# Signs of the weight words on VectorE, a folded factor for w_out, and layer 2's magnitude on ScalarE

## The chip, the cores and the metric

One core of one Trainium2 chip runs the whole program. The metric is device time in microseconds, the median of several runs. A profiled execution of the kernel before gives the trace that is read below. TensorE multiplies matrices, VectorE (DVE in the trace) and ScalarE (ACT) work on elements from PSUM and SBUF, GpSimd (POOL) on elements in SBUF, SyncE (SP) issues the DMAs.

## The reference

Attention over 4 batches, 8 heads, 576 positions and head size 64 (four heads see a local window of 32, four see every 32nd position), then two feed-forward layers over 2304 tokens of 512 values with 2048 hidden values each:

```python
attn = softmax(where(mask, q @ k.T / sqrt(64), -1e9)) ; x = attn @ v      # (2304, 512)
h = x @ moe_w_in  ; g = maximum(0.01 * h, h)                     ; x = g @ moe_w_out
h = x @ moe2_w_in ; g = maximum(h, 0) + log1p(exp(-abs(h)))      ; out = g @ moe2_w_out
```

q, k and v are float32. The four weights come as float64 and are read as pairs of 32-bit words.

## The kernel before

**Products.** Each operand of the feed-forward products is cut into a float16 high part and a float16 remainder, and a product is three matmuls (`mm3`, L462 to L464: high by high, high by remainder, remainder by high). Layer 1 runs over 8 units of 288 tokens: a first product (`plan_first`, pairs of 128 hidden rows) whose result ScalarE bends (L483) and casts (L486) and whose remainder GpSimd makes (L489), and a second product (`plan_second`, or for unit 0 `plan_second_by_f`, which goes along the hidden rows as the quarters of w_out come). Layer 2 runs over 9 units of 256 tokens, each in 8 steps k: first product, `size`, `relu`, `soft`, `add`, `sums`, `cut_high`, `cut_rest`, second product. Its second product uses seven products in place of eight, from sums of blocks.

**Weights.** A weight comes in four quarters of 2 MB, q = 0 to 3. `largest` (L156, VectorE) takes a quarter's largest magnitude, which goes over TensorE to all partitions and gives a scale. `low` (L162, VectorE) shifts the low words down by 29 bits, `shift` (L209, ScalarE) scales the high words, `merge` (L214, VectorE) joins both to a float32, `high` (L221, ScalarE) casts it to float16 and the remainder is the difference: `rest` (L226, on GpSimd for W1, on VectorE for W2) or `rest_of` (L230, VectorE). A sign bit has to be put into each low word before the merge: for W1 and O1 by ScalarE after the shift (`sign_of_scaled`, L205, float16 written with a stride of four), for W2 and O2 by VectorE before the shift (`sign`, L198). W1's and W2's quarters have a scale each (`plan_quarter`); O1's and O2's have one scale for all four quarters, so O1's conversion starts after its last quarter has come (`plan_together`). The loads of O1's quarters go into the areas that W1's quarters leave, one by one. The hidden values of layer 1 keep W1's four scales, and O1's quarters are multiplied with factors that even them out: `high` takes the factor as the scale of its cast, `rest_of` as the scalar of its difference.

**Layer 2's gate.** `size` (L1136, VectorE) clears the sign bit of h in PSUM, so SBUF holds the unscaled magnitude; `relu` (L1143, ScalarE) reads the same PSUM tile, after `size`, and frees it; `soft` (L1150, L1151, ScalarE) takes the exponent with the negative scales `nsc`, and then the logarithm.

**Order.** Every instruction is emitted by a planner (`Plan.run`): it keeps a clock for each engine, with a cost written beside each step, and one more clock, "port", for GpSimd's steps and the VectorE steps marked `port=True`. Among the steps that could start within 0.5 us of the earliest it takes the one of lowest rank. `RANKS` has an offset and a slope for each kind of step: A0 to A3 and B0 to B3 attention, L and LW and LO loads, W1r, W1m, O1r and O1m conversion, G0 to G2 first products of units 0 to 2, S0 to S2 their second products, M the later units, F, Fa, Fd, S, X and E layer 2. The order on each engine is fixed by this; at run time each engine goes through its queue in order. Where the plan sees TensorE free before 130 us it puts in filler matmuls (L92).

Of the kernel before, what the change touches and what calls it, by code (L numbers as in the profile page):

```python
# [10 lines left out]
F16 = mybir.dt.float16  # L11
F32 = mybir.dt.float32
I32 = mybir.dt.int32
U32 = mybir.dt.uint32
U16 = mybir.dt.uint16
AF = mybir.ActivationFunctionType
ALU = mybir.AluOpType
# [4 lines left out]
B, H, S, D = 4, 8, 576, 64  # L22
# [33 lines left out]
def build(tc, qt, kl, ks, v, wi1, wo1, wi2, wo2, mloc, mstr, out):  # L56
    nc = tc.nc
    with ExitStack() as ctx:
# [79 lines left out]
        flat = lambda y: y.rearrange("p a b -> p (a b)")  # L138


        class Weight:
# [60 lines left out]
            def sign_of_scaled(self, q):  # L202

                w = self.t[q].bitcast(F16).rearrange("p s (n t) -> p s n t", t=4)
                nc.scalar.activation(w[:, :, :, 1], self.words(q)[1].bitcast(F32), AF.Copy)  # L205

# [13 lines left out]
            def high(self, q, hl, by=1.0):  # L220
                nc.scalar.activation(flat(hl[0]), self.f[q], AF.Copy, scale=by)  # L221
                self.hl[q] = hl
# [4 lines left out]

            def rest_of(self, q, by):
                hi, lo = self.hl[q]
                nc.vector.scalar_tensor_tensor(  # L230
                    out=flat(lo), in0=self.f[q], scalar=by, in1=flat(hi), op0=ALU.mult, op1=ALU.subtract
                )
# [354 lines left out]
        W1, O1, W2, O2 = Weight("i1", wi1), Weight("o1", wo1), Weight("i2", wi2), Weight("o2", wo2)  # L587
# [26 lines left out]
        plan = Plan({"mm": 2, "sc": 1, "pt": 1, "po": 1, "s": 4, "a": 3, "t": 3, "qk": 5, "rs": 2, "x2": 2, "gr": RING, "ob": 2}, idle, 130.0)  # L614
# [85 lines left out]
        def plan_together(W, name, after, parts, then, w1):  # L700
# [6 lines left out]
            for q in range(4):  # L707
                ld = plan.add("SP", 5.9, lambda q=q: W.load(q, area(q)), after[q], ("L" + name, q))
                big = step("DVE", 2.2, lambda q=q: W.largest(q, m()[:, q : q + 1]), [ld], q)
                low = step("DVE", 1.14, lambda q=q: W.low(q), [ld], q + 0.1, port=True)  # L710
                loads.append(big)
                read.append([big, low])
# [15 lines left out]
            for q in range(4):  # L728
                y = step("ACT", 2.07, lambda q=q: W.shift(q, st["s"]), [t] + read[q], 4 + q)
                y = step("ACT", 1.9, lambda q=q: W.sign_of_scaled(q), [y], 4 + q)  # L730
                y = step("DVE", 2.2, lambda q=q: W.merge(q), [y], 4 + q, port=True)
                y = step("ACT", 1.85, lambda q=q: W.high(q, parts(q), O1.by[:, q : q + 1]), [y] + made[-1:] * (q % 2), 4 + q)
                made.append(
                    step("DVE", 2.3, lambda q=q: W.rest_of(q, O1.by[:, q : q + 1]), [y], 4 + q, port=True)
                )
            return made, scaled

        def plan_quarter(W, name, q, place, after, parts, after_read, then=None, eng="DVE"):
# [22 lines left out]
            if not then:  # L761
                y = step("DVE", 2.35, lambda: W.sign(q), [y], 0.2, port=True)
            y = step("ACT", 2.07, lambda: W.shift(q, st["s"]), [sc, x, y], 0.3)
            if then:
                y = step("ACT", 1.9, lambda: W.sign_of_scaled(q), [y], 0.3)
# [307 lines left out]
        class Unit:  # L1073
# [34 lines left out]
            def scales(self):  # L1108
                new = lambda n, t: sml.tile([P, n], F32, name=t, tag=t)
                self.sc, self.nsc = new(4, "x2s"), new(4, "x2n")  # L1110
# [3 lines left out]
                nc.vector.tensor_scalar(out=self.nsc, in0=self.sc, scalar1=-1.0, scalar2=None, op0=ALU.mult)  # L1114
# [19 lines left out]
            def size(self, k):  # L1134
                t = self.a[k] = tmp.tile([P, 2, U1], F32, name="t", tag="t")[:, :, :U2]
                nc.vector.tensor_scalar(  # L1136
                    out=t.bitcast(I32), in0=self.ps[k].bitcast(I32), scalar1=0x7FFFFFFF, scalar2=None, op0=ALU.bitwise_and
                )
# [9 lines left out]
            def soft(self, k):  # L1148
                a = self.a[k]
                nc.scalar.activation(a, a, AF.Exp, scale=self.nsc[:, k // 2 : k // 2 + 1])  # L1150
                nc.scalar.activation(a, a, AF.Ln, bias=1.0)  # L1151
# [75 lines left out]
        for u in range(NU2):  # L1227
# [9 lines left out]
            for k in range(NK):  # L1237
# [5 lines left out]
                size = plan.add("DVE", 0.6, bind(U.size), [g1], rank("Fd", k), take=["t"])  # L1243
# [96 lines left out]
```

## Time and profile before

| | us |
|---|---|
| median of 3 runs | 870.89 |
| runs | 870.03 to 873.74 |
| profiled execution | 871.47 |
| its span, first to last instruction | 869.5 |
| TensorE busy | 831.9 (96%) |
| VectorE busy | 533.7 (61%) |
| ScalarE busy | 528.3 (61%) |
| GpSimd busy | 265.0 (30%) |

The mean granted clock of TensorE is 0.995 of full speed. Busy time holds an instruction from its start to its end; where VectorE and GpSimd exclude each other, the time that one is held up lies in its duration. "L205" is line 205 of the kernel before.

### The profile page before, as it was taken

To read this page: it belongs to the slowest core of one execution; us is meant where nothing else is said; L and a number is where in the kernel's file an instruction comes from. 1 tells how busy PE (TensorE), PEld (TensorE's weight loads), DVE (VectorE), ACT (ScalarE), POOL (GpSimd) and SP (SyncE) were. 2 spreads that over 40 slices of the span, in tenths; PEclk is the share of its full clock that TensorE was granted. 3 is DMA by queue.
4 is the path that set the end of the run, shared out by engine and by line. 5 is a ranking of instruction groups with operands and counts; after the bars stand their busy time and mean duration, and the time that the engine had idled before them with its cause. 6 is when DMAs were issued, how large, how long until landed. Compare 5 with 4: busy or idle time off the path is not lost.

```text
span 869.5 us, 17639 instructions
## 1 busy us (share of the span) xinstructions
PE 831.9 (96%) x7330; PEld 684.6 (79%) x7330; DVE 533.7 (61%) x1232; ACT 528.3 (61%) x938; POOL 265.0 (30%) x194
## 2 busy tenths in 40 slices
PE   9888798799999999999999999999999999999997
PEld 5556576578777777787777777888888888888886
DVE  4895652542033535049647859977787778677684
ACT  5899979933456542263726457757575666657572
POOL 2365753120332124140504124323222322223131
PEclk9999999999999999999999999999999999999999
DMA  8932320121013470013221120000000000000000
GB/s 329 390 126 112 140 98 1 67 81 56 1 58 138 158 304 25 2 41 154 98 97 29 71 98 1 26 2 25 2 25 2 25 2 26 1 26 1 26 25 25
DMA packets 10991, 63.27 MB, mean 73 GB/s; under 512 B 1344, under 2 KB 1440, under 8 KB 7840
## 3 DMA queue, kind: packets, MB, share of 16 engines
q1 hardware_dynamic: 10656, 62.00, 19.0%
q8 instruction: 57, 0.93, 0.4%
q10 hardware_dynamic: 256, 0.16, 0.1%
q14 instruction: 22, 0.18, 0.1%
HBM read 57.44 MB, written 4.72 MB: 71 GB/s over the span
## 4 chain that ended last, share of the span: by engine, by line
PE 69%; ACT 12%; DVE 11%; DMA 3%; issue 3%; POOL 1%; SPq 0%; DVEq 0%; ACTq 0%; POOLq 0%
PE h L462 11%; PE h L464 11%; PE h L463 11%; PE o L462 10%; PE o L464 10%; PE o L463 10%; ACT pair L205 3%; ACT pair L209 2%; DMA pair<-wo_dram 2%; ACT s L368 2%; PE ps L322 2%; DVE pair L1005 2%; PE po L419 2%; PE pt L399 1%; ACT t L483 1%
## 5 line engine op out<-in xcount | busy, mean ns | idle before, releaser
L462 PE MATMUL h<-x,w 128*128 128x256 f16 (+1 forms) x1088 | 303.5, 279 | 7.2 <-ACT t L483 5.0
L464 PE MATMUL h<-x,w 128*128 128x256 f16 (+1 forms) x1088 | 303.4, 279 | 4.3 <-POOL w L226 4.3
L463 PE MATMUL h<-x,w 128*128 128x256 f16 (+1 forms) x1088 | 303.4, 279 | 0.0
L1155 POOL TENSOR_TENSOR pair<-pair,t 128x512 f32<-128x512 f32 x72 | 100.4, 1394 | 268.6 <-ACT t L1151 171.1
L489 POOL TENSOR_TENSOR g<-t,g 128x576 f16<-128x576 f32 x64 | 104.3, 1633 | 183.7 <-ACT g L486 181.7
L462 PE MATMUL o<-g,pair 128*128 128x288 f16 x512 | 147.7, 288 | 2.8 <-ACT pair L221 1.8
L464 PE MATMUL o<-g,pair 128*128 128x288 f16 x512 | 147.6, 288 | 2.5 <-DVE pair L230 2.5
L463 PE MATMUL o<-g,pair 128*128 128x288 f16 x512 | 147.5, 288 | 0.0
L463 PEld LDWEIGHTS <-w 128*128 128x128 f16 x1088 | 106.5, 98 | 27.3 <-issue 8.7
L464 PEld LDWEIGHTS <-w 128*128 128x128 f16 x1088 | 106.4, 98 | 24.3 <-POOL w L226 5.2
L462 PEld LDWEIGHTS <-w 128*128 128x128 f16 x1088 | 106.4, 98 | 19.4 <-issue 0.2
L1167 ACT ACTIVATE gr<-pair,x2b 128x896 f16<-128x896 f32 x72 | 74.0, 1038 | 57.2 <-DVE pair L1163 57.2
L1171 DVE SCALAR_TENSOR_TENSOR gr<-pair,x2b,gr 128x896 f16<-128x896 f32 x72 | 86.4, 1209 | 24.8 <-ACT gr L1167 24.7
L1163 DVE TENSOR_TENSOR pair<-pair 128x128 f32<-128x128 f32 x288 | 80.2, 324 | 16.8 <-POOL pair L1155 14.3
L1143 ACT ACTIVATE pair<-h,x2s 128x512 f32<-128x512 f32 x72 | 49.0, 680 | 60.0 <-DVE t L1136 54.4
L464 PE MATMUL o<-w,gr 128*128 128x256 f16 x306 | 83.4, 273 | 0.9 <-DVE gr L1171 0.7
L462 PE MATMUL o<-w,gr 128*128 128x256 f16 x306 | 83.4, 273 | 0.0
L463 PE MATMUL o<-w,gr 128*128 128x256 f16 x306 | 83.4, 273 | 0.0
L390 POOL TENSOR_TENSOR s<-s,sm 96x512 f32<-96x512 f32 (+3 forms) x48 | 43.7, 931 | 121.4 <-DVE sm L385 64.1
L483 ACT ACTIVATE t<-h,gs 128x576 f32<-128x576 f32 x64 | 47.0, 735 | 49.0 <-PE h L464 48.8
L1136 DVE TENSOR_SCALAR t<-h 128x512 int32<-128x512 int32 x72 | 48.7, 685 | 29.0 <-PE h L464 28.4
L214 DVE SCALAR_TENSOR_TENSOR pair<-pair 128x2048 int32<-128x2048 int32 x16 | 37.4, 2338 | 45.9 <-ACT pair L205 35.3
(123 smaller groups left out, 1391.1 us busy)
## 6 DMA issues: line engine op xcount, KB each, us to landing
pair<-wo_dram SPq DMA_DIRECT2D x12, 2048.0 KB, 7.8
pair<-wi_dram SPq DMA_DIRECT2D x8, 2048.0 KB, 10.1
out_dram<-pair SPq DMA_DIRECT2D x18, 256.0 KB, 2.2
q<-qt_dram SPq DMA_DIRECT2D x12, 288.0 KB, 5.9
v<-v_dram SPq DMA_DIRECT2D x2, 1408.0 KB, 7.7
pair<-v_dram SPq DMA_DIRECT2D x2, 1408.0 KB, 6.0
k<-ks_dram SPq DMA_DIRECT2D x7, 288.0 KB, 3.3
k<-kl_dram SPq DMA_DIRECT2D x5, 304.0 KB, 3.8
```

The lines of the kernel that those rows point to most:

```text
L390: nc.gpsimd.tensor_tensor(out=sv, in0=sv, in1=rs, op=ALU.mult)
L462: nc.tensor.matmul(ps, ah, bh, start=first, stop=False)
L463: nc.tensor.matmul(ps, ah, bl, start=False, stop=False)
L464: nc.tensor.matmul(ps, al, bh, start=False, stop=last)
L483: nc.scalar.activation(t, ps, AF.Prelu, scale=gates[f // 4], alpha=0.01)
L489: nc.gpsimd.tensor_tensor(out=g[:, 1, f : f + 2, :], in0=t, in1=g[:, 0, f : f + 2, :], op=ALU.subtract)
L1136: nc.vector.tensor_scalar(out=t.bitcast(I32), in0=self.ps[k].bitcast(I32), scalar1=0x7FFFFFFF, scalar2=None, op0=ALU.bitwise_and)
L1143: nc.scalar.activation(r[:, :4].rearrange("p (j h) n -> p j (h n)", j=2), self.ps[k], AF.Relu, scale=self.sc[:, k // 2 : k // 2 + 1],)
L1155: nc.gpsimd.tensor_tensor(out=r, in0=r, in1=self.a[k], op=ALU.add)
L1163: nc.vector.tensor_tensor(out=r[:, o], in0=r[:, x], in1=r[:, y], op=op)
L1167: nc.scalar.activation(self.a[k][:, 0], self.r[k][:, 1:], AF.Copy, scale=self.ag)
L1171: nc.vector.scalar_tensor_tensor(out=a[:, 1], in0=self.r[k][:, 1:], scalar=self.ag, in1=a[:, 0], op0=ALU.mult, op1=ALU.subtract)
```

## The change

Five things change. `sign_of_scaled` goes, and W1 and O1 get `sign` on VectorE between `low` and `shift` (for O1's last quarter with a rank behind the scale). For O1 `high` no longer takes the factor: a new ScalarE step `fold` multiplies the merged float32 in place, `high` casts the product, and `rest` on GpSimd takes the place of `rest_of` on VectorE. In layer 2 `size` becomes a Prelu with slope -1 on ScalarE that reads PSUM and applies the unit's scale, so that `soft` needs the scale -1.0 only and the vector `nsc` goes; its step now also waits for the unit's scales. All 36 entries of `RANKS` have new numbers.

```diff
-    "Fa": (61.151, 23.937), "Fd": (809.007, 5.868), "G1": (1158.664, 0.271), "O1m": (1374.727, 1.358),
-    "S0": (1133.607, 120.000), "W1m": (975.007, 5.818), "W1r": (1347.663, 2.158), ...
+    "Fa": (411.724, 0.050), "Fd": (63.172, 34.443), "G1": (1489.548, 0.577), "O1m": (1411.571, 1.167),
+    "S0": (376.286, 13.166), "W1m": (932.785, 55.840), "W1r": (1390.426, 33.062), ...
...
+            def fold(self, q, by):
+                nc.scalar.activation(self.f[q], self.f[q], AF.Copy, scale=by)
...
-                read.append([big, low])
+                sign = step("DVE", 2.35, lambda q=q: W.sign(q), [low], q + 0.2 + 0.86 * (q == 3), port=True)
+                read.append([big, sign])
...
                 y = step("ACT", 2.07, lambda q=q: W.shift(q, st["s"]), [t] + read[q], 4 + q)
-                y = step("ACT", 1.9, lambda q=q: W.sign_of_scaled(q), [y], 4 + q)
                 y = step("DVE", 2.2, lambda q=q: W.merge(q), [y], 4 + q, port=True)
-                y = step("ACT", 1.85, lambda q=q: W.high(q, parts(q), O1.by[:, q : q + 1]), [y] + made[-1:] * (q % 2), 4 + q)
-                made.append(step("DVE", 2.3, lambda q=q: W.rest_of(q, O1.by[:, q : q + 1]), [y], 4 + q, port=True))
+                y = step("ACT", 1.8, lambda q=q: W.fold(q, O1.by[:, q : q + 1]), [y], 4 + q)
+                y = step("ACT", 1.85, lambda q=q: W.high(q, parts(q)), [y] + made[-1:] * (q % 2), 4 + q)
+                made.append(step("Pool", 4.1, lambda q=q: W.rest(q, nc.gpsimd), [y], 4 + q))
...
-            if not then:
-                y = step("DVE", 2.35, lambda: W.sign(q), [y], 0.2, port=True)
+            y = step("DVE", 2.35, lambda: W.sign(q), [y], 0.2, port=True)
             y = step("ACT", 2.07, lambda: W.shift(q, st["s"]), [sc, x, y], 0.3)
-            if then:
-                y = step("ACT", 1.9, lambda: W.sign_of_scaled(q), [y], 0.3)
...
             def size(self, k):
-                nc.vector.tensor_scalar(out=t.bitcast(I32), in0=self.ps[k].bitcast(I32), scalar1=0x7FFFFFFF, ...
+                nc.scalar.activation(t, self.ps[k], AF.Prelu, scale=self.sc[:, k // 2 : k // 2 + 1], alpha=-1.0)
...
-                nc.scalar.activation(a, a, AF.Exp, scale=self.nsc[:, k // 2 : k // 2 + 1])
+                nc.scalar.activation(a, a, AF.Exp, scale=-1.0)
...
-                size = plan.add("DVE", 0.6, bind(U.size), [g1], rank("Fd", k), take=["t"])
+                size = plan.add("ACT", 0.6, bind(U.size), [g1, scaled], rank("Fa", k), take=["t"])
```

## Rows read from the trace of the kernel before

**Rows 1.** stretches, us: PE, PEld, DVE, ACT, POOL busy, clock, DMA, GB/s
```profile
53.20:154.60 101.40, 87.38 (x776) 67.72 (x777) 58.35 (x176) 91.51 (x143) 60.86 (x37) 1.00 0.26 96
...
154.60:177.80 23.20, 18.98 (x132) 13.87 (x132) 14.50 (x8) 23.17 (x40) 0.24 (x1) 0.85 0.18 63
...
177.80:500.00 322.20, 320.74 (x2780) 255.72 (x2778) 147.42 (x343) 149.19 (x309) 87.88 (x66) 1.00 0.24 88
...
500.00:550.00 50.00, 46.05 (x410) 39.57 (x409) 40.52 (x60) 31.59 (x41) 17.00 (x9) 1.00 0.12 43
...
550.00:862.50 312.50, 312.50 (x2865) 280.15 (x2863) 232.51 (x547) 194.07 (x269) 83.38 (x64) 1.00 0.04 15
```

**Rows 2.** what TensorE waited for: total us, times, longest
```profile
PE po L419 <- ACT a L407: 5.3, 5, 2.2
...
PE h L462 <- ACT t L483: 5.0, 5, 1.9
...
PE h L464 <- POOL w L226: 4.3, 3, 2.2
...
PE o L464 <- DVE pair L230: 2.5, 1, 2.5
```

**Rows 3.** groups by shape, ScalarE: busy us, mean ns | idle before
```profile
L205 ACT ACTIVATE pair<-pair 128x2048 f16<-128x2048 f32 x8 | 38.3, 4784 | 0.1
...
L209 ACT ACTIVATE pair<-pair,s 128x2048 f32<-128x2048 f32 x12 | 26.4, 2200 | 8.6 <-DVE s L188 8.5
...
L221 ACT ACTIVATE w<-pair 128x2048 f16<-128x2048 f32 x8 | 15.2, 1902 | 5.9 <-DVE pair L214 5.9
```

**Rows 4.** timeline, start and duration in us, stages A and B
```profile
49.09 4.08 POOL L226 TENSOR_TENSOR w<-pair,w 128x2048 f16<-128x2048 f32 x1 [10.13 <-ACT w L221]
...
105.65 4.09 POOL L226 TENSOR_TENSOR w<-pair,w 128x2048 f16<-128x2048 f32 x1 [0.18 <-ACT w L221]
...
127.11 2.18 ACT L209 ACTIVATE pair<-pair,s 128x2048 f32<-128x2048 f32 x1
...
175.48 2.34 DVE L230 SCALAR_TENSOR_TENSOR pair<-pair,by_o 128x2048 f16<-128x2048 f32 x1
```

**Rows 5.** single lines: count, ns min/median/max, first and last start
```profile
L162 DVE TENSOR_SCALAR pair<-pair x16: 1175/1226/2240, 32.0 to 509.4; 128x2048 uint32<-128x2048 uint32 x16
...
L198 DVE TENSOR_SCALAR pair<-pair x8: 2458/2466/3441, 328.9 to 520.0; 128x2048 uint16<-128x2048 uint16 x8
...
L214 DVE SCALAR_TENSOR_TENSOR pair<-pair x16: 2281/2293/3041, 44.7 to 526.4; 128x2048 int32<-128x2048 int32 x16
...
L226 POOL TENSOR_TENSOR w<-pair,w x4: 4065/4085/4102, 49.1 to 105.6; 128x2048 f16<-128x2048 f32 x4
...
L489 POOL TENSOR_TENSOR g<-t,g x64: 1273/1282/4447, 57.7 to 482.3; 128x576 f16<-128x576 f32 x64
...
L1155 POOL TENSOR_TENSOR pair<-pair,t x72: 1264/1272/3438, 508.7 to 851.2; 128x512 f32<-128x512 f32 x72
```

**Rows 6.** timeline at 520 us, VectorE and GpSimd
```profile
520.00 2.47 DVE L198 TENSOR_SCALAR pair<-pair 128x2048 uint16<-128x2048 uint16 x1
...
520.01 3.44 POOL L1155 TENSOR_TENSOR pair<-pair,t 128x512 f32<-128x512 f32 x1 [1.99 <-ACT pair L1143]
```

**Rows 7.** GpSimd lines in 53.2 to 110, 126 to 178, 53 to 178 us
```profile
L489 POOL TENSOR_TENSOR g<-t,g x11: 1282/1730/4447, 57.7 to 109.7; 128x576 f16<-128x576 f32 x11
...
L489 POOL TENSOR_TENSOR g<-t,g x7: 1277/1282/2201, 127.1 to 152.6; 128x576 f16<-128x576 f32 x7
...
L390 POOL TENSOR_TENSOR s<-s,sm x12: 545/1030/1039, 53.6 to 117.0; 96x512 f32<-96x512 f32 x6, 126x504 f32<-126x504 f32 x2, 108x432 f32<-108x432 f32 x2, 108x216 f32<-108x216 f32 x2
```

**Rows 8.** groups by shape, ScalarE and VectorE reading PSUM in both layers
```profile
L1143 ACT ACTIVATE pair<-h,x2s 128x512 f32<-128x512 f32 x72 | 49.0, 680 | 60.0 <-DVE t L1136 54.4 <-DVE gr L1171 4.7
...
L1136 DVE TENSOR_SCALAR t<-h 128x512 int32<-128x512 int32 x72 | 48.7, 685 | 29.0 <-PE h L464 28.4
...
L483 ACT ACTIVATE t<-h,gs 128x576 f32<-128x576 f32 x64 | 47.0, 735 | 49.0 <-PE h L464 48.8 <-POOL s L390 0.2
```

More of the change, by code (lines that the diff above doesn't have):

```diff
@@ L200, in sign @@
                 )
-            def sign_of_scaled(self, q):
-                w = self.t[q].bitcast(F16).rearrange("p s (n t) -> p s n t", t=4)
-                nc.scalar.activation(w[:, :, :, 1], self.words(q)[1].bitcast(F32), AF.Copy)
             def shift(self, q, s):
@@ L218, in merge, with high @@
                 self.f[q] = f.bitcast(F32)
-            def high(self, q, hl, by=1.0):
-                nc.scalar.activation(flat(hl[0]), self.f[q], AF.Copy, scale=by)
+            def fold(self, q, by):
+                nc.scalar.activation(self.f[q], self.f[q], AF.Copy, scale=by)
+            def high(self, q, hl):
+                nc.scalar.activation(flat(hl[0]), self.f[q], AF.Copy)
                 self.hl[q] = hl
@@ L226, in rest @@
                 eng.tensor_tensor(out=flat(lo), in0=self.f[q], in1=flat(hi), op=ALU.subtract)
[L228 to L232, printed above, removed]
             def scale_all(self, g):
@@ L729, in plan_together @@
                 y = step("ACT", 2.07, lambda q=q: W.shift(q, st["s"]), [t] + read[q], 4 + q)
-                y = step("ACT", 1.9, lambda q=q: W.sign_of_scaled(q), [y], 4 + q)
                 y = step("DVE", 2.2, lambda q=q: W.merge(q), [y], 4 + q, port=True)
-                y = step("ACT", 1.85, lambda q=q: W.high(q, parts(q), O1.by[:, q : q + 1]), [y] + made[-1:] * (q % 2), 4 + q)
-                made.append(
-                    step("DVE", 2.3, lambda q=q: W.rest_of(q, O1.by[:, q : q + 1]), [y], 4 + q, port=True)
-                )
+                y = step("ACT", 1.8, lambda q=q: W.fold(q, O1.by[:, q : q + 1]), [y], 4 + q)
+                y = step("ACT", 1.85, lambda q=q: W.high(q, parts(q)), [y] + made[-1:] * (q % 2), 4 + q)
+                made.append(step("Pool", 4.1, lambda q=q: W.rest(q, nc.gpsimd), [y], 4 + q))
             return made, scaled
@@ L1109, in scales @@
                 new = lambda n, t: sml.tile([P, n], F32, name=t, tag=t)
-                self.sc, self.nsc = new(4, "x2s"), new(4, "x2n")
+                self.sc = new(4, "x2s")
                 nc.vector.tensor_scalar(
@@ L1113, in scales @@
                 )
-                nc.vector.tensor_scalar(out=self.nsc, in0=self.sc, scalar1=-1.0, scalar2=None, op0=ALU.mult)
                 t = new(4, "x2b")
@@ L1135, in size @@
                 t = self.a[k] = tmp.tile([P, 2, U1], F32, name="t", tag="t")[:, :, :U2]
-                nc.vector.tensor_scalar(
-                    out=t.bitcast(I32), in0=self.ps[k].bitcast(I32), scalar1=0x7FFFFFFF, scalar2=None, op0=ALU.bitwise_and
-                )
+                nc.scalar.activation(t, self.ps[k], AF.Prelu, scale=self.sc[:, k // 2 : k // 2 + 1], alpha=-1.0)
             def relu(self, k):
```

20 rows, old and new, of the table RANKS are left out of this document.

## The prediction, made before the changed kernel ran

> **What bounds the kernel now.** I read the table of stretches first, then TensorE's waits, then the groups by shape, then the queues of the front in order of time. The stretches [rows 1] show a kernel that TensorE bounds almost everywhere: from 177.8 to 500 us it is busy 320.74 of 322.2 us, and from 550 to 862.5 us all 312.5. The time that can be won lies in three other places. From 53.2 us, where layer 1 starts in earnest, to 154.6 us TensorE is idle for 101.4 - 87.38 = 14.0 us; from 154.6 to 177.8 us for 4.2 us, with a granted clock of 0.85, which is worth at most 0.15 x 23.2 = 3.5 us more; from 500 to 550 us for 4.0 us. The rest, before 53.2 us and behind 862.5 us, is the start (loads and the first attention batch) and the last sums and store.
>
> In the first two of these stretches ScalarE is the engine that is never free: 91.51 of 101.4 us and 23.17 of 23.2 us [rows 1]. TensorE's waits say the same at second hand: it waits for ScalarE's fetches (L407), for its bends (L483), for GpSimd's remainders of W1 (L464 on L226), and for the last O1 remainder (L230) [rows 2], and the last two stand behind ScalarE in each quarter's chain. The reason is one line. The sign written by ScalarE (L205) takes 4.784 us for 128x2048, where the shift of the same words (L209) takes 2.20 and the cast (L221) 1.90 [rows 3]. There are 8 of them, 38.3 us, all for W1 and O1.
>
> So two stages decide the front. Stage A prepares the four quarters of W1: GpSimd's remainders start at 49.09 and, the last, at 105.65 us [rows 4], three spacings of 18.85 us. Stage B prepares O1: first shift at 127.11, last remainder done at 175.48 + 2.34 = 177.82 us [rows 4], 50.7 us. TensorE can't end unit 0's second product before the last quarter of O1 stands, and from there on it is saturated for 322 us, so what stage B's end moves, the end of the kernel moves.
>
> **The change part by part.** The sum is made against the profiled execution, 871.47 us with its span of 869.5 (2.0 us lie around it).
>
> *Signs.* ScalarE loses 8 x 4.78 = 38.3 us. VectorE gets 8 L198, which the trace has in later quarters at 2.47 us median [rows 5]: +19.7 us, between load and shift, beside the maximum's way over TensorE and back.
>
> *Fold.* ScalarE gets 4 in-place products of 128x2048 f32, an instruction the trace does not have. The nearest are L221 (contiguous, f16 out, 1.90) and L209 (f32 in and out, strided, 2.20) [rows 3]; I take 1.95, between them and nearer to the contiguous one, and keep both ends. A gain is excluded, it is an added pass. O1's remainder goes from VectorE (L230, 2.34) to GpSimd, where L226 of the same shape takes 4.09 [rows 4, 5]: VectorE -9.4, GpSimd +16.3 us.
>
> *What this does to the port.* Some VectorE instructions and GpSimd's exclude each other here. L1155 on GpSimd, 1.27 us as a rule, took 3.44 when it started at 520.01 beside the sign at 520.00 [rows 5, 6]: 2.17 us longer, nearly the sign's whole time. The same shows in the longest cases of L162 (2.24 against 1.23), L214 (3.04 against 2.29) and L489 (4.45 against 1.28) [rows 5]. So I count them as one resource, "the port". The change adds 19.7 + 16.3 - 9.4 = 26.6 us to it in the front, which is what eats most of ScalarE's 30.
>
> The Trainium skill, "SBUF — State Buffer", Who interferes with whom, would have it otherwise: a VectorE instruction with at most one SBUF input, outside the two-port modes, does not contend with GpSimd, and the sign has one input. If it ran outside those modes, 19.7 us would drop out of the port's sum and rival 1 would be the case. The trace disagrees: 3.44 us beside the sign against 1.27.
>
> *Stage A.* Quarter 0: shift, sign and cast before it were ScalarE's; without the 4.78, and with VectorE's 2.47 in front of the shift, its remainder starts 2.3 us earlier. That is -2.3. From there, per spacing, the port carries one remainder 4.09, one merge 2.29, one low word 1.23, 11/3 of L489 at 1.28 = 4.7 [rows 5, 7], and about 8 of the 12 attention products at 1.03 = 2.8 [rows 7]: 15.1 us of 18.85. The change adds O1's signs of the quarters that land meanwhile (two in three spacings, 1.6) and W1's own (0 if all three are done before 53 us, 2.47 if none is): 16.7 to 19.2. The bound engine of this stretch reaches 0.90 of it (ScalarE, 91.51 of 101.4 [rows 1]); at 0.90 the spacing is 18.6 to 21.3. I take 19.5: +0.65 x 3 = +2.0. ScalarE alone, if it set the spacing, would give 3 x 4.78 = 14.3 back; I count none of it, since the port takes over.
>
> *Stage B.* ScalarE's part falls by 4 x (4.78 - 1.95) = 11.3, to 39.4 us. The port carries 4 merges 9.2, 4 remainders 16.3, the last quarter's sign 2.5 (its rank puts it behind the scale) and 7 of L489 at 1.28, 9.0 [rows 5, 7]: 37.0, at 0.90 41.1. The port is the later: I take 42.0 and gain 50.7 - 42.0 = 8.7. The ends are 39.4 (a gain of 11.3) and 50.7 (none). The last quarter's remainder is longer by 1.75 than before, and that is in it.
>
> *Size on ScalarE.* 72 L1136 of 0.685 us leave VectorE, 72 Prelus of 128x512 from PSUM come to ScalarE; the Relu of the same tile (L1143) takes 0.680, which I take; the other bound is the Prelu of a larger tile (L483), 0.735 [rows 8]. From 550 to 862.5 us this makes ScalarE 194.07 + 64 x 0.68 = 237.6 of 312.5 us, 76% [rows 1], under a saturated TensorE: nothing, as long as its queue serves the size within the time of a second-product group. If it doesn't, each k could lose up to one size, 0.68 x 72 = 49 us; as a saturated stretch has shown no wait at all with ScalarE at 62%, I put it near nothing. What is queued behind a size are Relu and exponent of the same k, which needed the unit's scales before; so the added wait for the scales delays nobody new. From 500 to 550 us VectorE is busy 40.52 of 50 and TensorE idle 4.0 [rows 1]; about 9 of the sizes lie there, 6 us off VectorE. I take 2.5 of the 4.0 back, bounds 0 and 4.0. The second scale vector that goes (one small instruction per unit) is worth nothing: it has the unit before as cover.
>
> *Ranks.* They set which of several ready instructions is queued first. I give them no price; their bounds are those of the rivals.
>
> Sum: -2.3 + 2.0 - 8.7 - 2.5 = -11.5; 871.5 - 11.5 = 860.0. The profiled execution stands 0.6 above the median of 870.89, which is inside what I can tell; I forecast 860.
>
> **The rivals.** *1. The port does not bind, TensorE runs through.* For it: ScalarE really is freed of 30 us; against it: the 3.44 us of [rows 6] and a port filled to 15.1 of 18.85. Then of the 14.0 + 4.2 idle and the 3.5 of clock, 21.7 together, some 18 come back, with 2.3 ahead of them and 2.5 later on: 871.5 - 22.8 = 849.
>
> *2. The gain is given back before layer 2.* O2's four quarters go through one area one after the other, and VectorE is busy 0.81 of 500 to 550 us [rows 1]. If that chain hangs on loads and VectorE and not on TensorE, an earlier TensorE waits there for as long as it came earlier: only the 2.5 of freed VectorE stays, 869. Against it: O2's conversion begins behind layer 1's own work.
>
> *3. Slower: GpSimd's queue holds the front.* Its place is 50 to 180 us. If W1's signs all fall into stage A, the spacing becomes 21.3, and with the remainders of 4.09 in front of the bends' remainders (three t buffers, so TensorE stops after three pairs) I add 1.5: 22.8, 3 x 3.95 = +11.9 less quarter 0's 2.3. In stage B O1's four remainders then stand before the same L489s, and its 8.7 are gone. 871.5 + 9.6 = 881, less the part of layer 2's start that still comes back, of which I count 1 here: 880. It decides where the port's demand passes 18.85 us a quarter at the share it reaches, about 17 us of work. For it: 16.7 to 19.2 lies on both sides of that; against it: the order written out knows the port and the ranks can let unit 1 wait.
>
> **How the numbers follow.** A half per cent, 4.4 us, is about what a measurement of this kernel can tell from no change: faster is below 866.5, slower above 875.2. My forecast has 0.38 (its own range 853 to 868), rival 1 0.14, rival 2 0.24, rival 3 0.24. Faster: 0.14 and nearly all of 0.38, 0.50. Same: 0.25. Slower: 0.25. The range that leaves out 2 in 10 goes from rival 1's 849 less a us to just below rival 3's 880: 848 to 879.
>
> **What would show it.** Right: no L205; L198 x16 at about 2.5; the last O1 remainder, now on GpSimd, ending near 169 us; ScalarE no longer full in 53 to 178; more of the L489s far above their 1.28, since they wait beside signs; TensorE still without gaps behind 550. Stage A is wrong if GpSimd's W1 remainders stand 15 us apart (rival 1) or 22 (rival 3). Rival 2 shows as more than 4 us of TensorE idle between 480 and 550. The prediction fails altogether if TensorE waits for the new size in layer 2, or if an attention batch comes late in 200 to 500 by the new ranks.

## The result, and the profile after

| | before | after |
|---|---|---|
| median of 9 runs, us | 872.74 | 863.99 |
| runs, us | 870.03 to 875.94 | 862.26 to 868.51 |
| profiled execution, us | 871.47 | 863.87 |
| its span, us | 869.5 | 862.1 |
| TensorE busy, us | 831.9 | 836.1 |
| mean granted clock | 0.995 | 0.983 |

The ratio is 0.9907, 95% interval [0.9889, 0.9925]: faster by 0.9%, and 4 us above the forecast of 860. The span fell by 7.4 us: TensorE's idle time (span less busy) went from 37.6 to 26.0 us, its busy time rose by 4.2 us. Filler matmuls count as busy, but both kernels spend the same on them (21.5 and 21.6 us), so the idle time that went is real.

The stretches of the kernel after, columns as in [rows 1] with start and end ahead:

```profile
0.00:37.00 37.00, 30.25 (x230) 18.97 (x230) 22.40 (x42) 19.21 (x84) 8.78 (x14) 0.86 0.92 357
37.00:56.70 19.70, 19.53 (x122) 11.43 (x123) 17.23 (x49) 12.96 (x44) 10.89 (x5) 0.83 0.30 127
56.70:117.50 60.80, 53.21 (x495) 42.29 (x494) 56.33 (x151) 49.06 (x132) 44.37 (x24) 0.94 0.37 134
117.50:140.00 22.50, 20.56 (x168) 15.82 (x166) 18.32 (x45) 16.89 (x38) 18.95 (x12) 0.92 0.39 147
140.00:177.50 37.50, 37.50 (x311) 30.12 (x309) 15.14 (x23) 33.42 (x44) 32.19 (x15) 1.00 0.11 40
177.50:500.00 322.50, 321.97 (x2789) 257.20 (x2787) 145.89 (x319) 143.65 (x289) 82.53 (x59) 1.00 0.23 85
500.00:550.00 50.00, 46.91 (x423) 40.91 (x422) 37.39 (x60) 42.20 (x60) 15.56 (x11) 1.00 0.11 41
550.00:855.00 305.00, 305.00 (x2796) 273.53 (x2795) 190.59 (x466) 217.81 (x321) 80.39 (x61) 1.00 0.04 15
```

And the first three and the fifth of these stretches in the kernel before:

```profile
0.00:37.00 37.00, 32.97 (x269) 19.89 (x269) 24.40 (x54) 22.49 (x102) 9.64 (x15) 1.00 0.90 349
37.00:56.70 19.70, 15.68 (x128) 9.79 (x128) 16.43 (x57) 17.35 (x44) 8.07 (x7) 1.00 0.55 211
56.70:117.50 60.80, 51.23 (x465) 39.79 (x463) 37.73 (x104) 59.31 (x106) 43.58 (x25) 1.00 0.39 147
...
140.00:177.50 37.50, 29.99 (x228) 22.20 (x226) 21.76 (x26) 37.37 (x48) 7.79 (x4) 0.91 0.11 40
```

Read for each stretch TensorE's busy time against its length. From 140 to 177.5 us 7.5 us of idle time are gone and the clock is full: the largest gain of any stretch. ScalarE fell from 59.31 to 49.06 us in 56.7 to 117.5 and VectorE rose from 37.73 to 56.33, so VectorE now fills 0.93 of that stretch. The start got worse (idle 4.0 to 6.75 us in the first 37), and the clock, full before, is 0.83 to 0.94 up to 140 us. The 500 to 550 stretch is almost as idle as in [rows 1], 3.1 us for 4.0.

Stages A and B, timeline of the kernel after (start and duration in us; the first two lines ran at the same time; in brackets the idle time of the engine before the instruction, and what ended it):

```profile
50.32 2.46 DVE L198 TENSOR_SCALAR pair<-pair 128x2048 uint16<-128x2048 uint16 x1
50.45 6.15 POOL L224 TENSOR_TENSOR w<-pair,w 128x2048 f16<-128x2048 f32 x1 [5.17 <-ACT w L219]
...
68.69 4.08 POOL L224 TENSOR_TENSOR w<-pair,w 128x2048 f16<-128x2048 f32 x1
85.52 4.07 POOL L224 TENSOR_TENSOR w<-pair,w 128x2048 f16<-128x2048 f32 x1
...
102.44 1.89 ACT L219 ACTIVATE w<-pair 128x2048 f16<-128x2048 f32 x1
...
112.39 1.05 POOL L382 TENSOR_TENSOR s<-s,sm 108x216 f32<-108x216 f32 x2 [3.51 <-DVE sm L377]
113.40 4.09 POOL L224 TENSOR_TENSOR w<-pair,w 128x2048 f16<-128x2048 f32 x1
...
131.44 2.22 ACT L204 ACTIVATE pair<-pair,s 128x2048 f32<-128x2048 f32 x1
...
173.38 4.10 POOL L224 TENSOR_TENSOR pair<-pair 128x2048 f16<-128x2048 f32 x1 [0.79 <-ACT pair L219]
```

Against [rows 4]: W1's first remainder starts at 50.45 for 49.09 and the last ends at 117.49 for 109.74, a spacing of (113.40 - 50.45) / 3 = 20.98 for 18.85. That is a mean of 18.2, 16.8 and 27.9: only the last quarter is late. Its cast ended at 104.33, and its remainder stood 9 us longer in GpSimd's queue, behind attention products (L382), one of which waited 3.5 us for VectorE. O1's conversion starts at 131.44 for 127.11 and ends at 177.48 for 177.82: 46.0 us long for 50.7, and finished at the same time as before.

So TensorE runs through 140 to 177.5 although its operands come no earlier. What it ran there, groups by shape, the kernel after and then the kernel before:

```profile
L454 PE MATMUL h<-x,w 128*128 128x288 f16 x53 | 15.2, 286 | 0.0
L454 PE MATMUL o<-g,pair 128*128 128x288 f16 x48 | 13.7, 286 | 0.0
...
L391 PE MATMUL pt<-ident,s 96*128 96x96 f32 x8 | 1.0, 245 | 0.0
```

```profile
L462 PE MATMUL o<-g,pair 128*128 128x288 f16 x40 | 12.6, 314 | 2.8 <-ACT pair L221 1.8 <-DVE mx L345 1.1
...
L462 PE MATMUL h<-x,w 128*128 128x288 f16 x31 | 8.9, 286 | 2.2 <-ACT t L483 2.2
```

First products (h) need no quarter of O1. The new order has 53 of each of the three left for this stretch, the old one 31. At the rate of the stretch after (311 products in 37.5 us, 0.12 us each) the 22 x 3 more are some 8 us, about the idle time that went. The old gaps were waits for O1's conversion (1.8 and 2.5), for the bend (2.2) and for an attention maximum (1.1).

TensorE's longest waits in the kernel after (total us, times, longest):

```profile
PE pt L391 <- ACT a L399: 4.3, 5, 1.8
PE ps L314 <- DVE mx L337: 3.9, 3, 1.8
PE pm L122 <- DVE m L257: 2.7, 1, 2.7
...
PE h L454 <- ACT t L475: 1.9, 1, 1.9
```

Of [rows 2] the waits for GpSimd's remainders of W1 (4.3) and for the last O1 remainder (2.5) are gone from the list altogether, and the waits for the bend fell from 5.0 to 1.9. What is left at its head is attention: the maximum (L337, L257) and the exponents on ScalarE (L399).

The new forms, groups by shape of the kernel after (busy us, mean ns | idle before):

```profile
L198 DVE TENSOR_SCALAR pair<-pair 128x2048 uint16<-128x2048 uint16 x16 | 47.9, 3007 | 0.2
```

```profile
L1123 ACT ACTIVATE t<-h,x2s 128x512 f32<-128x512 f32 x72 | 48.8, 678 | 50.5 <-PE h L456 50.5
...
L216 ACT ACTIVATE pair<-pair,by_o 128x2048 f32<-128x2048 f32 x4 | 8.0, 1988 | 0.0
```

The fold's 1.99 us and the size's 0.678 are what the prediction took (1.95 and 0.68). The sign's mean of 3.01 for 2.47 I put down to waiting for GpSimd, which the duration contains (experiment 4 shows a case).

### The profile page after: what moved, and what is told of

It is laid out like the page before. It is cut to its first block, busy times and chain, and to the rows that moved or that the text cites. A ratio compares the mean times of both kernels' runs of the same rounds, so it can differ in the third digit from the quotient of the medians.

```text
span 862.1 us, 17623 instructions
## 1 busy us (share of the span) xinstructions
PE 836.1 (97%) x7328; PEld 691.0 (80%) x7328; DVE 506.2 (59%) x1155; ACT 535.7 (62%) x1006; POOL 293.7 (34%) x198
## 3 DMA queue, kind: packets, MB, share of 16 engines
q1 hardware_dynamic: 10656, 62.00, 19.2%
## 4 chain that ended last, share of the span: by engine, by line
PE 80%; DVE 8%; ACT 6%; POOL 2%; DMA 2%; issue 1%; SPq 0%; DVEq 0%; ACTq 0%; POOLq 0%
PE h L454 12%; PE o L454 12%; PE h L455 12%; PE h L456 12%; PE o L456 12%; PE o L455 12%; PE po L411 2%; PE ps L314 2%; PE pt L391 2%; PE idle L92 2%; POOL pair L224 1%; DVE pair L198 1%; DVE pair L209 1%; ACT s L360 1%; DMA v<-v_dram 1%
## 5 line engine op out<-in xcount | busy, mean ns | idle before, releaser
L1140 POOL TENSOR_TENSOR pair<-pair,t 128x512 f32<-128x512 f32 x72 | 96.0, 1337 | 271.5 <-ACT pair L1128 145.1
L481 POOL TENSOR_TENSOR g<-t,g 128x576 f16<-128x576 f32 x64 | 111.4, 1746 | 184.0 <-ACT g L478 181.6
L382 POOL TENSOR_TENSOR s<-s,sm 96x512 f32<-96x512 f32 (+3 forms) x48 | 51.4, 1092 | 87.6 <-DVE sm L377 69.4
L1123 ACT ACTIVATE t<-h,x2s 128x512 f32<-128x512 f32 x72 | 48.8, 678 | 50.5 <-PE h L456 50.5
L454 PEld LDWEIGHTS <-pair 128*128 128x128 f16 x512 | 50.0, 98 | 12.8
L456 PEld LDWEIGHTS <-pair 128*128 128x128 f16 x512 | 50.0, 98 | 12.7
```

Of the source, the lines that this page charges most:

```text
L382: nc.gpsimd.tensor_tensor(out=sv, in0=sv, in1=rs, op=ALU.mult)
L454: nc.tensor.matmul(ps, ah, bh, start=first, stop=False)
L456: nc.tensor.matmul(ps, al, bh, start=False, stop=last)
L481: nc.gpsimd.tensor_tensor(out=g[:, 1, f : f + 2, :], in0=t, in1=g[:, 0, f : f + 2, :], op=ALU.subtract)
L1123: nc.scalar.activation(t, self.ps[k], AF.Prelu, scale=self.sc[:, k // 2 : k // 2 + 1], alpha=-1.0)
L1140: nc.gpsimd.tensor_tensor(out=r, in0=r, in1=self.a[k], op=ALU.add)
```

## The experiments

Each kernel was timed beside the kernel before, whose medians there were 872.7 to 873.4 us. Intervals are of 95%, for the ratio to the kernel before.

**1. What the ScalarE signs cost.** The kernel before, with their instruction left out.

```diff
             def sign_of_scaled(self, q):
-                w = self.t[q].bitcast(F16).rearrange("p s (n t) -> p s n t", t=4)
-                nc.scalar.activation(w[:, :, :, 1], self.words(q)[1].bitcast(F32), AF.Copy)
+                pass
```

> The kernel before with the 8 sign instructions of ScalarE (L205) left out, so the low words keep no sign; the queue order of every other instruction stays as it is. Theory (ScalarE's 38.3 us of signs set the front): the W1 remainders on GpSimd come 15 to 16 us apart in place of 18.85, O1's conversion takes about 35 us in place of 50.7, and the time falls to 850 to 858. Rival (the shared port sets stage A already, only O1's stage is ScalarE's): spacing stays at 17.5 or more, and the time falls by about 8 only, to 862 to 866.

853.67 us, ratio 0.9787 [0.9763, 0.9812], 19 us. GpSimd's W1 remainders and the last O1 remainder on VectorE in its timeline:

```profile
46.88 4.07 POOL L225 TENSOR_TENSOR w<-pair,w 128x2048 f16<-128x2048 f32 x1 [7.59 <-ACT w L220]
...
99.19 4.09 POOL L225 TENSOR_TENSOR w<-pair,w 128x2048 f16<-128x2048 f32 x1
```

```profile
156.45 2.35 DVE L229 SCALAR_TENSOR_TENSOR pair<-pair,by_o 128x2048 f16<-128x2048 f32 x1
```

The spacing is 17.4 us, not the 15 to 16 that was expected, but stage B ends at 158.80, 19.0 earlier than in [rows 4], and the span is 850.4, 19.1 shorter. The end of stage B and the end of the kernel moved together, one to one, as the premise of the prediction has it. That does not show that the one carries the other: the last W1 remainder also ended 6.5 us earlier here, so the whole front moved.

**2. What the signs cost on VectorE.** The kernel after, with most of each of W1's and O1's signs left out.

```diff
+                if self.name in ("i1", "o1"):
+                    w = w[:, :, :128]
```

> The changed kernel with its 8 new VectorE signs (W1 and O1) done over a quarter of the words, about 0.65 us in place of 2.47, in the same queue order; the other words keep no sign. Theory (the signs hold the port and VectorE's queue, and cost the front): the W1 remainders on GpSimd come 19 us apart or less in place of 20.98, quarter 0's remainder no longer takes 6.15, and the time falls by 4 to 7 against the changed kernel, to 857 to 860. Rival (TensorE has spare work, unit 1's first product, so stage A's length costs nothing): spacing shrinks but the time stays within 1.5 of 864.

The slice leaves 256 of 2048 words, an eighth and not the quarter that was meant:

```profile
50.62 0.45 DVE L200 TENSOR_SCALAR pair<-pair 128x256 uint16<-128x256 uint16 x1
```

861.24, ratio 0.9862 [0.9845, 0.9878]: 2.75 us less than the kernel after, between the two expectations, so about 2.75 x 8/7 = 3.1 for whole signs if it goes by length (an estimate). The first W1 remainder lasts 4.14 for 6.15, but the spacing only falls to 20.5 (17.2, 16.8 and 27.4). The signs on VectorE are cheap, and they are not what holds stage A at 21 us. Stage B ends at 175.08, 2.4 us earlier than in the kernel after, and the span is 859.6, 2.5 shorter.

**3. The clock at the start.** The kernel after with filler products where TensorE first falls idle.

```diff
+                t = ps_pt.tile([P, 512], F32, name="pm", tag="pt")
+                if self.b == 1:
+                    for _ in range(12):
+                        nc.tensor.matmul(t..., idb, idb..., start=True, stop=True)
...
```

> The changed kernel with 12 filler matmuls of 512 columns put in TensorE's queue just ahead of the transposition of batch 1's maximum, where it waits 2.67 us at 24 us; nothing else is moved. Theory (the low clock of 0.50 from 28 to 41 us delays the first attention batch and with it everything behind): the granted clock stays 1.00 in 24 to 44 us, quarter 0's remainder comes 3 us earlier, the time falls to 860 to 862. Rival (quarter 0 is set by its load, which lands at 34 us, and by VectorE's queue): the clock stays up, but the remainder moves by less than 1 us and the time by less than 1.5, 863 to 865.

864.72, ratio 0.9903 [0.9888, 0.9917]. The clock of the first 37 us rose from 0.86 to 0.93, W1's first remainder came at 49.98 for 50.45, and no time was gained. The rival's numbers came out, but the clock did not stay up, as both expectations had assumed. It was 0.94 or more until 32 us, and then the half clock came all the same: 0.50 from 32 to 40, where the kernel after has it from 28 to 40:

```profile
32.00:36.00 4.00, 3.61 (x24) 2.48 (x22) 3.97 (x4) 2.57 (x11) 1.28 (x2) 0.50 0.95 369
```

What a full clock through the whole start would give was not measured by it.

**4. Old ranks with new steps.** The kernel after with the `RANKS` of the kernel before, all 37 entries.

```diff
-    "A0": (1254.691, 0.078), "A1": (1428.142, 11.747), ...
+    "A0": (904.756, 0.733), "A1": (1181.967, 5.007), ...
```

> The changed kernel with the ranks of the kernel before; everything else as in the change, so the queues are ordered anew. Theory (the gain comes from moving the signs, fold and size, the ranks only settle ties): within 4 us of the changed kernel, 860 to 868. Rival (the order, above all unit 1's first product kept as spare work for the time in which O1 is made, carries the gain): no gain left, 870 to 876.

918.81, ratio 1.0527 [1.0511, 1.0542]. Neither expectation held: it is 55 us slower than the kernel after. Two stretches and TensorE's two longest waits:

```profile
117.50:140.00 22.50, 11.13 (x80) 8.51 (x81) 11.55 (x26) 8.65 (x24) 8.68 (x8) 0.64 0.38 132
...
177.50:200.00 22.50, 7.66 (x60) 6.38 (x60) 7.67 (x28) 20.97 (x44) 19.40 (x7) 0.50 0.25 83
```

```profile
PE pt L391 <- ACT a L399: 20.2, 10, 15.3
PE ps L314 <- DVE mx L337: 16.9, 4, 14.2
```

TensorE stands 11.4 and 14.8 us in these two stretches, at 0.64 and 0.50 of the clock. It waits in attention, single waits of 15.3 and 14.2 us, with other products queued behind. What it waits for stands in a queue as well:

```profile
111.25 9.64 DVE L198 TENSOR_SCALAR pair<-pair 128x2048 uint16<-128x2048 uint16 x1
...
166.24 6.40 ACT L204 ACTIVATE pair<-pair,s 128x2048 f32<-128x2048 f32 x3
```

The maximum (L337) comes on VectorE at 126.72, behind a sign of O1 that lasted 9.64 us because GpSimd was busy without a gap until 118.6. The fetch (L399) comes on ScalarE at 185.91, behind 19.8 us of O1's conversion that begin at 166.24. The O1 remainders start at 176.5 to 193.4.

**5. New ranks with old steps.** The other corner: the kernel before with the new `RANKS`.

```diff
-    "A0": (904.756, 0.733), "A1": (1181.967, 5.007), ...
+    "A0": (1254.691, 0.078), "A1": (1428.142, 11.747), ...
```

> The kernel before with the RANKS of the change and nothing else. Of the 8.7 us between the kernels, 19.2 less 3.7 are signs; that sum overshoots, and what the new order does is so far a remainder. Theory (an order fits only the steps it was made for: with the ScalarE sign at 4.78 us, which the plan carries at 1.9, and O1's remainder on VectorE, the new order meets late operands): 885 to 915 us, TensorE with gaps of over 8 us in 117 to 200. Rival (the new order is better or worse by itself, through the spare products that it keeps for 140 to 177.5 us, whatever makes the signs): within 862 to 880 us, no gap in 140 to 177.5.

920.64, ratio 1.0543 [1.0527, 1.0558]; even slower than expected. Its stretch of stage B and its longest wait:

```profile
140.00:177.50 37.50, 15.08 (x124) 11.79 (x122) 18.52 (x67) 37.18 (x65) 7.11 (x8) 0.68 0.15 49
```

```profile
PE po L419 <- DMA pair<-v_dram: 14.8, 1, 14.8
```

ScalarE is full (37.18 of 37.5), three ScalarE signs (14.3 us) among its work, but it was as full in the kernel before (37.37). TensorE waits 14.8 us, to 180.03, for a load of attention values that was issued only at 173.69. Why the load is late was not followed up. So the four corners are 873 (old, old), 919 (new steps, old ranks), 921 (old steps, new ranks) and 864 (new, new). Neither set of ranks is better by itself; each fits its own steps.

**6. Layer 2's part, in either order.** First the kernel before with the size on ScalarE at the same places.

```diff
-                nc.vector.tensor_scalar(out=t.bitcast(I32), in0=self.ps[k].bitcast(I32), scalar1=0x7FFFFFFF, ...)
+                nc.scalar.activation(t, self.ps[k], AF.Prelu, alpha=-1.0)
```

> The kernel before with its size step done by ScalarE (a Prelu of slope -1 from PSUM, unscaled) at the same places of the emission order; nothing else is changed, so this is the layer-2 part of the change alone. Theory (ScalarE has room, VectorE's relief at the start of layer 2 brings a little): ScalarE at 76% from 550 us on without a gap on TensorE, idle of 500 to 550 us down from 4.0 to 1 to 3, the time 1 to 3 below the kernel before. Rival (a size queued behind a cast that waits for VectorE holds PSUM): TensorE waits for ScalarE's Relu in layer 2, the time 3 or more above the kernel before.

872.39, ratio 1.0004 [0.9993, 1.0014]: nothing. The idle time of 500 to 550 fell from 4.0 to 2.9, and behind 550, where [rows 1] had none, it is 1.5:

```profile
500.00:550.00 50.00, 47.13 (x427) 41.35 (x426) 32.99 (x55) 37.40 (x53) 13.52 (x9) 1.00 0.12 43
550.00:862.50 312.50, 310.99 (x2841) 277.79 (x2839) 193.06 (x479) 220.93 (x329) 83.12 (x63) 1.00 0.04 15
```

Then the kernel after with the size back on VectorE, unscaled, and the exponent with the negative scales. The planner puts its steps in order again, with the VectorE rank.

```diff
...
-                nc.scalar.activation(t, self.ps[k], AF.Prelu, scale=self.sc[:, k // 2 : k // 2 + 1], alpha=-1.0)
+                nc.vector.tensor_scalar(out=t.bitcast(I32), in0=self.ps[k].bitcast(I32), scalar1=0x7FFFFFFF, ...)
...
-                size = plan.add("ACT", 0.6, bind(U.size), [g1, scaled], rank("Fa", k), take=["t"])
+                size = plan.add("DVE", 0.6, bind(U.size), [g1], rank("Fd", k), take=["t"])
```

> The changed kernel with layer 2's size back on VectorE, unscaled, and the exponent with the negative scale vector; only this part is undone, the ranks stay those of the change. Theory (layer 2's part is worth nothing in this kernel as well, since 500 to 550 us came out at 3.1 us idle for 4.0, and behind 550 TensorE is full either way): 863 to 866 us, TensorE idle 3 to 4 us in 500 to 550. Rival (with 0.84 of ScalarE and 0.75 of VectorE busy in 500 to 550 the move is what keeps O2's conversion ahead of TensorE): 866.5 us or more, idle of 5 us or more between 480 and 560.

869.7, ratio 0.9958 [0.9942, 0.9975]: 5.7 us above the kernel after. My theory fell. The rival has the size of it but not all of the place: 3.1 us are idle in 500 to 550 as in the kernel after, and 4.5 us more in 550 to 700, where the kernel after has none. That stretch, and the wait in 500 to 700:

```profile
550.00:700.00 150.00, 145.48 (x1325) 129.43 (x1323) 112.22 (x271) 92.11 (x125) 38.25 (x29) 1.00 0.04 15
```

```profile
PE h L454 <- ACT pair L1131: 6.8, 8, 2.0
```

A first product waits for the Relu (L1131), which frees h in PSUM and which itself follows the size. In the new order the move of the size is worth 5.7 us, in the old one nothing. What the placement alone does and what the rank, which this edit also changes, was not told apart.

**7. Fold and GpSimd remainder.** The kernel after, the cast with the factor again and O1's remainder on VectorE, in the same order.

```diff
-                nc.scalar.activation(self.f[q], self.f[q], AF.Copy, scale=by)
+                pass
...
-                nc.scalar.activation(flat(hl[0]), self.f[q], AF.Copy)
+                nc.scalar.activation(flat(hl[0]), self.f[q], AF.Copy, scale=O1.by[:, q : q + 1] if self.name == "o1" else 1.0)
...
```

> The changed kernel with its fold left out of the emission: O1's cast takes the factor as its scale and the remainder is made by VectorE with the factor, as in the kernel before, at the same places of the emission order; signs, size and ranks stay as in the change. ScalarE loses 8.0 us, GpSimd 16.4, VectorE gains 9.4. Theory (TensorE is saturated from 140 us on, so O1's later quarters are not waited for): O1's last remainder ends 5 to 8 us earlier, the time stays within 1.5 of the changed kernel, 862 to 865. Rival (fold and GpSimd's remainders set the end of the front): the time falls by 5 or more, to 859 or less.

863.64, ratio 0.9896 [0.9879, 0.9914]. Stage B ends at 174.14 for 177.48, 3.3 us earlier, and the median time is 0.35 us less. The profiled span is 1.3 us shorter (860.8), but at a clock of 0.988 for 0.983; a run of this kernel at 0.983 spans 862.4, where the kernel after has 862.1. TensorE had no wait for O1 left to lose, so in the new order the end of stage B, moved by itself, does not move the end of the kernel. (In experiment 2 both moved by 2.4 to 2.5 us, but there more than stage B had changed.)

**8. Quarter 0 of W1.** In the kernel after two 2 MB loads of W1 are issued together, and quarter 0's `largest` starts at 34.03 for 29.79. Here quarter 1's load is issued behind batch 1's third pair of heads.

```diff
+                    if o.rank == ("LW1", 1):
+                        later = o
+                    else:
+                        o.fn()
+                    if o.rank == ("L1", 3):
+                        later.fn()
```

> The changed kernel with the load of W1's second quarter issued behind the loads of batch 1's third head pair, as in the kernel before, so the first quarter has the DMA engines nearly for itself; all other queues as in the change. Theory (the first quarter is late because two 2 MB loads issued together land together at 34 us in place of 29.8): its largest starts 3 to 5 us earlier, the first remainder and with it all W1 follows by 2 to 4, the time falls to 860 to 862. Rival (the VectorE queue and attention set the first quarter): the load lands earlier, the remainder moves by less than 1 us, the time stays at 863 to 865.

863.61, ratio 0.9892 [0.9877, 0.9906], with `largest` at 34.41 and the remainder at 50.83: no earlier. From 30 to 31 us the DMA engines stood still (share 0.00), so quarter 0 had landed by then, while VectorE went through attention's steps until 34.41. The load was not what it waited for; the rival held. With the edit of experiment 7 added:

> Both of the two edits above in one kernel, whose output is the reference's: first quarter's load alone, no fold, O1's remainder on VectorE with the factor. Theory (only the first edit matters): as the kernel with that edit alone, within 1 us, 860 to 862. Rival (they add up, since O1's quarters are waited for once W1 comes earlier): 2 us or more below the better of the two.

862.66, ratio 0.9882 [0.9866, 0.9899], 1.3 us below the kernel after; the two intervals overlap, so this is not told apart.

**9. An order for measured durations.** The steps of the last run, with the later W1 loads put behind batch 1's loads in the plan itself; the planner's costs of the long steps set to what the trace shows; new ranks, found by trying many sets against this plan.

```diff
...
-            HOP, SLACK, LOAD = 0.2, 0.5, 0.9
+            HOP, SLACK, LOAD = 0.2, 0.5, 1.8
...
-                sign = step("DVE", 2.35, ...
+                sign = step("DVE", 2.47, ...
...
-                y = plan.add("DVE", 0.83, bind(U.sums), [y], rank("Fd", k), port=True)
+                y = plan.add("DVE", 1.1, bind(U.sums), [y], rank("Fd", k), port=True)
...
```

> The changed kernel without the fold (the cast takes the factor and VectorE makes O1's remainder, as in the run without a fold), W1's second load behind batch 1's head-pair loads, the planner's costs of the long VectorE and ScalarE steps set to the measured means (sign 2.47, shift 2.19, merge 2.29, sums 1.1, exponent with logarithm 1.3, a load's latency 1.8), and new ranks for these costs. Theory (the order is the largest term, and one made for the durations that the trace shows brings the idle time of 56 to 140 us down from 9 to 4 us and keeps the clock up): 852 to 859 us. Rival (the plan does not know the clock, and an order made for its costs gives as good a fit by chance as the one before): 860 to 872 us.

858.69, ratio 0.9837 [0.9824, 0.9850]. The theory's range held, its reason only in part: from 56.7 to 140 us TensorE is idle 7.2 us for 9.5, not 4, at a clock of 0.96 for 0.94. Then another set of ranks for the same plan, nothing else changed:

> The kernel of the run with measured costs with another set of RANKS, whose planned end is 858.4 us where the first set's was 861.5 (measured 858.7); no other line differs. Theory (the plan with measured durations follows the chip, so that a plan shorter by 3 us is shorter there too): 854 to 857.5 us, TensorE idle below 20 us in the span for 22.0. Rival (what is left of the gap between plan and chip is clock and load times, which the plan does not know, and a shorter plan is as often longer there): 858 to 864 us.

854.08, ratio 0.9788 [0.9764, 0.9811]: the best version, 1.1% below the kernel after, at a granted clock of 0.999. It leaves no work out, and stands where experiment 1 came by leaving the signs out. Its front:

```profile
0.00:37.00 37.00, 33.05 (x273) 19.95 (x274) 25.15 (x56) 22.75 (x103) 12.09 (x18) 1.00 0.68 261
37.00:56.70 19.70, 17.88 (x177) 11.29 (x174) 16.28 (x79) 18.98 (x72) 8.20 (x6) 1.00 0.57 229
56.70:117.50 60.80, 59.58 (x508) 44.88 (x509) 57.59 (x126) 47.13 (x112) 46.83 (x25) 1.00 0.57 214
...
140.00:177.50 37.50, 36.98 (x311) 29.39 (x309) 29.38 (x35) 20.86 (x33) 18.63 (x8) 1.00 0.24 86
```

VectorE carries as much in 56.7 to 117.5 as in the kernel after (57.59 for 56.33), and TensorE is idle 1.2 us there for 7.6. The span's idle time is 852.0 - 835.0 = 17.0 us for 26.0. But most of this is not time won, since the fillers (L92) count as busy. The planner put 116 of them into this kernel, 78 into the kernel after. In 56.7 to 117.5, where the kernel after has none, they are:

```profile
56.70:117.50 60.80, 8.60 (x36) 3.43 (x36) 1.00 0.57 214
```

Idle time and fillers together are 17.0 + 30.7 = 47.7 us for 26.0 + 21.6 = 47.6 in the kernel after. What is shorter is the busy time of the other matmuls, 7250 in both kernels: 835.0 - 30.7 = 804.3 us for 836.1 - 21.6 = 814.5, at a granted clock of 0.999 for 0.983. A filler's end overlaps the next matmul, which makes these sums uncertain by some 2 us. So 8 to 10 of the 10 us between the two kernels stand in how fast the products ran, not in waits. What kept the clock up is open: the fillers, the costs and the ranks all changed, no run had the fillers alone in these places, and no set of ranks searched as long with the old costs was run.

## Why the prediction was right, and where its steps were not

The direction was right, and so was the idle time: the sum of -11.5 us was made as if all of it were waiting, and TensorE's idle time fell by 11.6. The busy time, for which the sum had no term, took 4.2 back, so the profiled time fell by 7.6. And most terms behind the sum were wrong, so the agreement of -11.5 and -11.6 is partly luck.

*Signs off ScalarE.* Right, and larger than priced. Experiment 1 gives 19 us for L205 in the old order. The prediction counted on the port to eat most of that; experiment 2 puts VectorE's signs at about 3.1 us. The two do not add up: 19.2 - 3.1 is 16, and the whole change gave 8.75. Each was measured in another order.

*The port.* That the sign and GpSimd exclude each other was right: 6.15 us beside a sign of 2.46, where the remainder takes 4.09 alone and 4.14 beside an eighth of a sign (0.45 us). The Trainium skill, "SBUF — State Buffer", Who interferes with whom, has a one-input VectorE instruction leave GpSimd alone only outside the two-port modes. No run here shows in which mode the sign ran, so these rows and [rows 6] show the exclusion; that they disagree with the page, as the prediction has it, is not shown.

*Stage A.* Forecast -2.3 for quarter 0 and a spacing of 19.5. Quarter 0 came 1.4 later and the spacing was 20.98; the last remainder ended 7.75 us later, not 0.3 earlier. The mean is close to rival 3's 21.3, but the signs on the port are not its reason (experiment 2): two spacings, 18.2 and 16.8, lie below the range of 18.6 to 21.3, and the third, 27.9, holds 9 us in GpSimd's queue. Rival 3's price is missing too: TensorE's idle time in 56.7 to 117.5 fell from 9.6 to 7.6 us all the same.

*Stage B.* The length was 46.0 for the forecast 42.0, and it began 4.3 later, so its end moved by 0.3 us and not by 8.7. The step that failed is "what stage B's end moves, the end of the kernel moves". In the old order experiment 1 fits it (19.0 and 19.1 us); in the new one it does not hold (3.3 us earlier in experiment 7, and 0.35 in the median time). The gain of that stretch, 7.5 us of idle time and the clock back from 0.91 to 1.00, came with the first products that the new order keeps for it; the counts say so, and no run took them away by themselves.

*Size on ScalarE.* Forecast 2.5 us back in 500 to 550; 0.86 came, and behind 550 TensorE stayed full as forecast. The move is worth nothing at the old places (experiment 6), and taking it back, with its rank, costs 5.7 us in the new order.

*Ranks.* "I give them no price" was the largest miss. Exchanged against the steps, either way, they cost 47 to 55 us, and from the steps of the last run of experiment 8 another set with other costs gave 8.6 more (862.66 to 854.08). What of the front they set by themselves is only partly shown. The low clock of the first 56.7 us comes with the new ranks, also with the old steps (0.87 and 0.81 in experiment 5's kernel, 0.95 and 1.00 in experiment 4's). Stage A's late start does not go by the ranks alone: with the old ranks and the new steps the first remainder starts at 51.25. Nor does the spare work in stage B, which is missing with the new ranks and the old steps.

*Clock.* The sum had no term for it, and it is the difference between 860 and 864 as far as the busy time shows. These are 4 us windows of the kernel after:

```profile
20.00:24.00 4.00, 4.00 (x58) 3.22 (x58) 1.36 (x3) 3.99 (x18) 0.39 (x1) 1.00 1.03 437
24.00:28.00 4.00, 1.33 (x10) 1.02 (x10) 3.54 (x4) 2.10 (x11) 0.00 (x0) 0.83 1.03 440
28.00:32.00 4.00, 3.39 (x28) 2.40 (x24) 3.26 (x13) 1.07 (x2) 2.63 (x3) 0.50 0.96 370
...
40.00:44.00 4.00, 4.00 (x15) 1.94 (x12) 3.49 (x16) 2.16 (x5) 2.73 (x2) 0.54 0.71 301
```

TensorE stood 2.7 us in 24 to 28, and its clock was 0.50 of full, the level of 1.2 GHz, until after 40. With later dips (0.58 in 80 to 88, 0.79 in 120 to 128) the mean fell from 0.995 to 0.983. Without the fillers both kernels run 7250 matmuls, and their busy time rose from 831.9 - 21.5 = 810.4 to 814.5 us. The nine runs of the kernel after go the same way: the span is 860.5 us at a clock of 0.989 and 866.7 at 0.979. The dip at the start does not seem to set stage A: in experiment 7's execution, whose front is the same, the clock was 1.00 again from 32 to 36 us, and the first remainder started at 50.29. What each later dip costs was not measured.

*Rivals.* Rival 1 failed on the spacing (21, not 15). Rival 2 failed: 3.1 us idle in 500 to 550, no more than before. Rival 3 had its spacing as a mean, but neither its reason (experiment 2 leaves most of the signs out, and the spacing stays at 20.5) nor its time.

## What to carry to other kernels

Where an order was written out for a set of steps, the steps and the order are one change. Neither tells much without the other (864 and 873 us together, 919 and 921 exchanged), and a part's worth can be 0 in one order and 5.7 us, there with its rank, in the other. Ask of a late operand not only when it comes but what else the bound engine has ready then: O1, ready at the same time, cost 4.3 us of waits in one order and none in the next. And where fillers run, take them out of TensorE's busy time before you read its idle time as a gain: the best version has 9 us less idle time than the kernel after and 7 to 9 us more fillers, and most of its gain is in products that ran at a higher clock. The old plan carried a step of 4.78 us at 1.9; whether measured costs by themselves make a better order was not told apart.

## What the hardware showed that I had not expected

ScalarE needs 4.78 us to write 128x2048 f16 values eight bytes apart, for 2.20 with a strided f32 and 1.90 with contiguous f16 output [rows 3]. And a stand of 2.7 us at 24 us was followed by some 12 us at half the clock, in which TensorE was busy 3.0 to 3.8 of every 4 us. It need not last that long: experiment 7's kernel, with the same front, stood 4.0 us there and had 0.57 from 28 to 32 us, then 1.00, 0.85 and 0.72 in the three windows up to 44.
